# Layer 5's residual adds as accumulating DMAs in a deep-and-cross network, with later output transposes and x0 loads

## The chip, the core and the metric

The kernel runs on one core of a Trainium2 chip. The metric is the device time of one execution in microseconds (us). The core has TensorE (PE: matmuls; its weight loads are shown apart as PEld), VectorE (DVE), ScalarE (ACT), GpSimd (POOL) and SyncE (SP). In this kernel SP issues nearly all DMAs and POOL a few; 16 DMA engines carry them.

## The reference

```python
B, D, L = 16384, 1024, 6                       # bf16
x = x0
for l in range(L):
    proj = jnp.einsum('bd,de->be', x, ws[l]) + bs[l]
    x = x0 * proj + x
return x
```

Six layers. Each multiplies 16384 rows by a 1024 by 1024 matrix, adds a bias, multiplies by the untouched input x0 and adds x, the residual.

## The kernel before

**Tiles.** The 16384 rows go through in 16 pairs of 1024 rows (a pair is two blocks of 512, n = 0 and 1). A unit is one layer of one pair, 96 units in all, worked in the order pair 0 layers 0 to 5, pair 1 layers 0 to 5, and so on. x and x0 are held transposed in SBUF, features on the partitions: `x0Ts[pr % 2]` and `xsts[pr % 2]`, two buffers of each that the pairs use in turn. A quadrant (dh, n) of such a tile, `blk(t, dh, n)`, is 512 features of one block: 128 partitions by 2048 elements, 4 KB a partition, 512 KB.

**Fewer products.** A unit is a 2 by 2 block product done in Winograd's form with seven products. Differences of x are made by VectorE (T1 to T4), combinations of weight blocks ("5", "6", "7", "3", and inner ones "5i", "2i") too, but only in pair 0: POOL saves them to the DRAM tensor `Lc` (line 306) and later pairs load them from there. Pair 0 and the last unit use one level of this; all other units split two of the seven products again (`inner`, line 411).

**Evacuation.** TensorE sums into PSUM banks `pA[m]` and `pX[m]`. ScalarE moves them on: `F.m` copies pA[m] into pX[m], on which product 3 then builds (P3.m needs F.m); `E3.m` writes U, `E7.m` writes V, `E4.m` writes W, all with the bias (line 298); Q comes from E2 or from the inner products' copies (line 294). Q, U, V and W are tiles `ev2` to `ev5`, one buffer each, used again by every unit: the next unit's first E3 writes U's buffer again.

**Tail of a unit.** VectorE finishes each quadrant (line 202 is the helper `tt`): an add (Ua, Va), a product with x0 (Qm, Um, Vm, and Wma and Wmb in halves) and the residual add into xst (Qa, Ux, Vx, Wx; line 457). In the last unit of all, another branch finishes the quadrants in smaller pieces, with its own transposes and stores.

**Output and input of a pair.** After layer 5 SP transposes block n of xst into the same pair's x0T by DMA (`tro`, line 538), which needs both quadrants of block n (Q and W for n = 0, U and V for n = 1), and then stores x0T to `out` (`sto`, line 544). The next-but-one pair uses the same buffers. The x0 of the next pair is loaded into the other x0T by two transposing DMAs (`ld`, line 533).

**Order.** The program order of every engine is written by ranks. Each operation has a rank in us, its unit's base (23.4 us a unit, 24.2 in pair 0 and in the last) plus a number from a table (`EARLY` for the first units, `R2` for the rest). A heap takes the operation of lowest rank whose operands are already placed. Every engine runs its own list in that order, and waits by semaphores. Weights go through a ring of 16 tiles of 512 KB: after each placed operation, `pump` places as many loads on SP's list as the ring has free tiles, so an SP load waits for TensorE to finish with an old tile. A unit of pair 1 and later loads nine tiles.

Of the kernel before, what the change touches and what calls it, by code (L numbers as in the profile page):

```python
# [9 lines left out]
ADD = mybir.AluOpType.add  # L10
# [138 lines left out]
def kernel(  # L149
# [7 lines left out]
    nc = tc.nc  # L157
    P = nc.NUM_PARTITIONS
    B, D = x0.shape
    L = ws.shape[0]  # L160
# [3 lines left out]
    NB = 512  # L164
    PR = 2 * NB
    assert D == 1024 and B % PR == 0
    NPAIR = B // PR
# [15 lines left out]
    x0Ts = [work.tile([P, 2, KD, NB], BF16, name=f"x0T{i}") for i in range(2)]  # L183
# [5 lines left out]
    P1s, P5s, Q, U, V, W = (work.tile([P, KH, NB], BF16, name=f"ev{i}") for i in range(6))  # L189
# [8 lines left out]
    def blk(t, dh, n):  # L198
        return t[:, n, dh * KH:(dh + 1) * KH, :]

    def tt(o, a, b, op):
        nc.vector.tensor_tensor(out=o, in0=a, in1=b, op=op)  # L202
# [61 lines left out]
    def op(rank, fn, rd=(), wr=(), weights=()):  # L264
        for k in weights:
            uses_left[k] = uses_left.get(k, 0) + 1
        ops.append((rank, fn, tuple(rd), tuple(wr), tuple(weights)))

    base = 0.0
    QD = ((0, 0), (0, 1), (1, 0), (1, 1))  # L270
    for u, (pr, l) in enumerate(units):
        one, first, last = level1(u), u == 0, u == NU - 1
        rk = {**SAVES, **EARLY[u]} if u < len(EARLY) else (RLAST if last else R2)
        x0T, xst = x0Ts[pr % 2], xsts[pr % 2]
        xs = x0T if l == 0 else xst
        X0 = {q: f"x0.{pr % 2}.{q[0]}{q[1]}" for q in QD}
        XO = {q: f"xs.{pr % 2}.{q[0]}{q[1]}" for q in QD}
        XI = X0 if l == 0 else XO

        def add(name, fn, rd=(), wr=(), weights=(), rk=rk, base=base, u=u):  # L280
            op(base + rk[name], fn, rd, wr, [(u, w) for w in weights])

        def ttop(name, o, a, b, o_, rd, wr, **kw):
            add(name, lambda: tt(o, a, b, o_), rd, wr, **kw)
# [16 lines left out]
        if pr == 0:  # L301
# [32 lines left out]
            for X, s in (("2i", isum[2 * (l % 2)]), ("5i", isum[2 * (l % 2) + 1])):  # L334
                a = lambda r, c, X=X, u=u: wt[(u, X[0])][:, r * KQ:(r + 1) * KQ, c * HQ:(c + 1) * HQ]
# [37 lines left out]
        if not one:  # L373
            for X, Bm, src in (("5", T[1][:], "T1"), ("2", B21, XI[1, 0])):
                q = lambda dh, n, Bm=Bm: Bm[:, dh * KQ:(dh + 1) * KQ, n * NQ:(n + 1) * NQ]
# [15 lines left out]
        if not one:  # L391
            for X, Bm, src, a, b, C in (("5", T[1][:], "T1", 0, 1, P5s), ("2", B21, XI[1, 0], 2, 3, Q)):
                q = lambda dh, n, Bm=Bm: Bm[:, dh * KQ:(dh + 1) * KQ, n * NQ:(n + 1) * NQ]
# [50 lines left out]
        allm = lambda s: [f"{s}.{m}" for m in range(KH)]  # L444
        if not one:
            ttop("Q1", Q[:], Q[:], P1s[:], ADD, allm("Q") + allm("P1s"), allm("Q"))
        if not last:
            ttop("Ua", U[:], U[:], P5s[:], ADD, allm("U") + allm("5c"), allm("U"))
            ttop("Va", V[:], V[:], P5s[:], ADD, allm("V") + allm("5c"), allm("V"))
            for nm, C, q in (("Q", Q, (0, 0)), ("U", U, (0, 1)), ("V", V, (1, 1)), ("W", W, (1, 0))):  # L450
                if nm == "W":
                    for h, g in enumerate("ab"):
                        sl, ms = slice(h * KQ, (h + 1) * KQ), [f"W.{2 * h}", f"W.{2 * h + 1}"]
                        ttop("Wm" + g, C[:, sl], C[:, sl], blk(x0T, *q)[:, sl], MULT, ms + [X0[q]], ms)
                else:
                    ttop(nm + "m", C[:], C[:], blk(x0T, *q), MULT, allm(nm) + [X0[q]], allm(nm))
                ttop(nm + ("a" if nm == "Q" else "x"), blk(xst, *q), C[:], blk(xs, *q), ADD, allm(nm) + [XI[q]], [XO[q]])
        else:

# [24 lines left out]
            for m in range(KH - 1):  # L484
# [3 lines left out]
                out=W[:, KH - 1, :], in0=pA[KH - 1][:], scalar=b_all[:, c:c + 1], in1=blk(x0T, 1, 0)[:, KH - 1, :], op0=ADD, op1=MULT),  # L488
# [3 lines left out]
            for nm, src, dst, r, c0, c1 in outs:  # L492
                add("tr" + nm, lambda src=src, dst=dst: nc.sync.dma_start_transpose(
                    out=dst.rearrange("p j k r -> p (j k) r"), in_=src.rearrange("r j k p -> r (j k p)")),
# [30 lines left out]
        for f in late:  # L525
            f()
        nxt = pr + 1
        if l == (2 if pr == 0 else 0) and nxt < NPAIR:
            for n in range(2):
                XN = [f"x0.{nxt % 2}.{d}{n}" for d in range(2)]  # L530

                def ld(n=n, nxt=nxt):
                    nc.sync.dma_start_transpose(out=x0Ts[nxt % 2][:, n], in_=x0[nxt * PR + n * NB:nxt * PR + (n + 1) * NB, :])
                op(base + 23 + n, ld, [], XN)
        if l == L - 1 and not last:
            for n in range(2):
                def tro(n=n, x0T=x0T, xst=xst):
                    nc.sync.dma_start_transpose(out=x0T[:, n].rearrange("p k (j r) -> p (k j) r", r=P),
                                                in_=xst[:, n].rearrange("r k b -> r (k b)"))
                op(base + (28 if n == 0 else 31), tro, [XO[0, n], XO[1, n]], [X0[0, n], X0[1, n]])  # L540

                def sto(n=n, x0T=x0T, pr=pr):
                    with nc.allow_non_contiguous_dma(reason="256B runs"):
                        nc.sync.dma_start(out[pr * PR + n * NB:pr * PR + (n + 1) * NB, :].rearrange("(j p) (k r) -> p k j r", p=P, r=P),
                                          x0T[:, n].rearrange("p k (j r) -> p k j r", r=P))
                op(base + (42 if n == 0 else 45), sto, [X0[0, n], X0[1, n]], ["out"])
        base += SPAN0 if one else SPAN2


# [95 lines left out]
```

## Time and profile before

| | |
|---|---|
| median of 3 runs | 2271.25 us (2270.97 to 2272.67) |
| profiled execution: span from first to last instruction | 2269.4 us |
| TensorE busy | 2248.5 us, 99% of the span |
| VectorE busy | 2092.1 us, 92% |
| ScalarE busy | 1847.8 us, 81% |
| POOL busy | 24.5 us, 1% |
| mean granted TensorE clock | 1.000 |
| SP's DMA queue | 534.58 MB, 78.6% of 16 engines' span |
| POOL's DMA queue | 19.93 MB, 2.3% |
| weight load, issue to landing (median) | 4.7 us from Lc, 5.2 us from ws |
| Lc save by POOL, issue to landing (median) | 6.1 us and 6.8 us |
| output transpose, issue to landing (median) | 7.3 us |

The span leaves out what lies around the first and last instruction, 1.85 us against the median. In rows of the timeline the columns are the start in us, the length in us, the engine, the line, the operation, what is written and read, and the number of merged instructions; in brackets stands idle time before it and what ended it. A row of waits gives the total in us, the number and the longest. A window's row gives its length and the busy time of each engine, then the granted clock, the share of the DMA engines and their rate. Neighbouring instructions on an engine overlap a little, so from start to start a VectorE add takes 1.13 us where its own length is 1.22 us.

### The profile page before, as it was taken

The numbers are of one execution on the slowest core, as the hardware profiler recorded it, in microseconds if no ns is written. First come the engines' busy times: TensorE is split into PE (matmuls) and PEld (weight loads), VectorE is DVE, ScalarE is ACT, GpSimd is POOL, SyncE is SP. The second block draws the span as 40 slices with busy tenths as digits, with TensorE's granted clock in tenths as the row PEclk, the third lists the DMA queues.
The fourth block names the chain that finished last, engine by engine and source line by source line (L and its number), as shares of the span: only waits on it lengthen the run. The fifth ranks groups of instructions, "written<-read, shape, count | busy, mean of one in ns | idle before, by whom it ended". The sixth has DMA issues, their size and how long they took to land.

```text
span 2269.4 us, 34750 instructions
## 1 busy us (share of the span) xinstructions
PE 2248.5 (99%) x12754; PEld 1267.4 (56%) x12993; DVE 2092.1 (92%) x2331; ACT 1847.8 (81%) x3234; POOL 24.5 (1%) x46
## 2 busy tenths in 40 slices
PE   9999999999999999999999999999999999999998
PEld 4455555555555555555555555555555555555554
DVE  8999999999999999999999999999999999999997
ACT  6678888888888888888888888888888888888887
POOL 1110000000000000000000000000000000000000
PEclk9999999999999999999999999999999999999999
DMA  8779797796977969779697796977969689696872
GB/s 279 229 270 301 251 249 264 220 303 206 251 259 224 288 220 248 264 218 288 215 266 251 227 285 205 277 242 227 288 201 294 225 225 294 195 295 224 236 247 66
DMA packets 620492, 557.02 MB, mean 245 GB/s; under 512 B 391456, under 2 KB 546592, under 8 KB 620320
## 3 DMA queue, kind: packets, MB, share of 16 engines
q1 hardware_dynamic: 614240, 534.58, 78.6%
q0 software_dynamic: 5488, 19.93, 2.3%
q8 instruction: 102, 1.67, 0.3%
q14 instruction: 70, 0.57, 0.1%
q10 hardware_dynamic: 592, 0.27, 0.0%
HBM read 437.79 MB, written 52.43 MB: 216 GB/s over the span
## 4 chain that ended last, share of the span: by engine, by line
PE 99%; issue 1%; DMA 0%; ACT 0%; SPq 0%; DVE 0%; ACTq 0%
PE pA L289 58%; PE pX L411 24%; PE pX L289 17%; DMA ev<-in_x_dram 0%; ACT pX L294 0%; PE pA L505 0%; PE pX L359 0%; PE pX L505 0%; DVE x0T L516 0%; ACT ev L294 0%; ACT x0T L363 0%; ACT ip L294 0%; SPq L577 0%; SPq L574 0%; ACTq L294 0%
## 5 line engine op out<-in xcount | busy, mean ns | idle before, releaser
L289 PEld LDWEIGHTS <-wp 128*128 128x128 bf16 x7904 | 772.9, 98 | 838.1 <-issue 0.9
L289 PE MATMUL pA<-T,wp 128*128 128x512 bf16 x4468 | 1033.0, 379 | 7.3
L298 ACT ACTIVATE ev<-pA,b_all 128x512 bf16<-128x512 f32 x1123 | 717.5, 692 | 211.2 <-PE pA L289 164.0
L411 PEld LDWEIGHTS <-wp 128*128 128x128 bf16 x4984 | 487.7, 98 | 151.5 <-issue 0.2
L202 DVE TENSOR_TENSOR ev<-ev,x0T 128x2048 bf16<-128x2048 bf16 (+2 forms) x483 | 483.0, 1002 | 8.1 <-ACT ev L298 1.5
L202 DVE TENSOR_TENSOR ev<-ev,ev 128x2048 bf16<-128x2048 bf16 (+1 forms) x283 | 343.9, 1216 | 71.7 <-ACT ev L298 44.6
L202 DVE TENSOR_TENSOR xst<-ev,xst 128x2048 bf16<-128x2048 bf16 x319 | 389.1, 1220 | 19.1 <-PE pX L289 0.9
L411 PE MATMUL pX<-ti,wp 128*128 128x256 bf16 x2848 | 397.8, 273 | 0.0
L298 ACT ACTIVATE ev<-pX,b_all 128x512 bf16<-128x512 f32 x412 | 285.4, 697 | 63.8 <-PE pX L289 62.9
L289 PE MATMUL pX<-xst,wp 128*128 128x512 bf16 x1371 | 323.3, 379 | 0.3
L289 PE MATMUL pA<-xst,wp 128*128 128x512 bf16 x1205 | 302.4, 379 | 3.9
L294 ACT CAST ev<-pX 128x512 bf16<-128x512 f32 x384 | 232.1, 606 | 47.9 <-ACT ev L298 37.4
L294 ACT COPY pX<-pA 128x512 f32<-128x512 f32 x412 | 237.5, 602 | 21.7 <-PE pA L289 18.7
L294 ACT COPY pX<-pX 128x512 f32<-128x512 f32 x356 | 207.8, 584 | 8.6 <-ACT ip L294 0.2
L202 DVE TENSOR_TENSOR T<-xst 128x2048 bf16<-128x2048 bf16 x160 | 195.0, 1218 | 0.3
L202 DVE TENSOR_TENSOR T<-xst,T 128x2048 bf16<-128x2048 bf16 x160 | 195.0, 1219 | 0.2
L294 ACT CAST iu<-pX 128x512 bf16<-128x512 f32 x356 | 192.7, 601 | 0.0
L202 DVE TENSOR_TENSOR ev<-iu,ip 128x1024 bf16<-128x1024 bf16 x178 | 123.2, 692 | 60.7 <-ACT iu L294 60.7
L411 PE MATMUL pX<-T,wp 128*128 128x256 bf16 x1068 | 160.2, 273 | 0.0
L294 ACT CAST ip<-pX 128x512 bf16<-128x512 f32 x178 | 104.7, 589 | 54.0 <-PE pX L411 54.0
L411 PE MATMUL pX<-xst,wp 128*128 128x256 bf16 x888 | 133.2, 273 | 0.1
L202 DVE TENSOR_TENSOR xst<-ev,x0T 128x2048 bf16<-128x2048 bf16 x64 | 78.3, 1223 | 1.6
(50 smaller groups left out, 636.4 us busy)
## 6 DMA issues: line engine op xcount, KB each, us to landing
wp<-Lc SPq DMA_DIRECT2D x538, 512.0 KB, 4.7
wp<-in_ws_dram SPq DMA_DIRECT2D x287, 512.0 KB, 5.2
out_dram<-x0T SPq DMA_DIRECT2D x30, 1024.0 KB, 8.8
Lc<-wp POOLq DMA_DIRECT2D x24, 512.0 KB, 6.1
Lc<-isum POOLq DMA_DIRECT2D x12, 512.0 KB, 6.8
w<-in_ws_dram SPq DMA_DIRECT2D x5, 512.0 KB, 6.1
ev<-in_x_dram SPq DMA_DIRECT2D x3, 512.0 KB, 7.2
out_dram<-x0T SPq DMA_DIRECT2D x3, 256.0 KB, 4.2
```

Of the source, the lines that this page charges most:

```text
L202: nc.vector.tensor_tensor(out=o, in0=a, in1=b, op=op)
L289: nc.tensor.matmul(bank[:], lhsT=wt[(u, w)][:, k, m * P:(m + 1) * P], rhs=rhs[:, k, :], start=(start and k == 0), stop=(k == KH - 1), skip ...
L294: add(name, lambda: nc.scalar.copy(out=dst, in_=src), rd, wr)
L298: add(name, lambda: nc.scalar.activation(out=dst, in_=src, func=IDENT, bias=b_all[:, c:c + 1], scale=1.0), rd, wr)
L411: nc.tensor.matmul(pX[bank][:, m * NQ:(m + 1) * NQ], lhsT=wv[:, k, m * P:(m + 1) * P], rhs=rhs[:, k, :], start=(start and m == 0 and k == ...
```

## The change

In layer 5 of every pair but the last one, the residual add of each of the four quadrants is no VectorE instruction any more. POOL issues a DMA from the product tile (Q, U, V or W) onto the quadrant of xst, which adds as it writes (`accum_op=ADD`). It takes the rank of the add that it replaces. The two output transposes move from ranks 28 and 31 to 37 and 46, the two stores from 42 and 45 to 53 and 63. The two loads of the next pair's x0, which stood together in layer 2 (pair 0, ranks 23 and 24) or layer 0 (later pairs, ranks 23 and 24), are placed one in layer 2 and one in layer 3, at rank 23 of the layer in pair 0 and at rank 6 in later pairs.

```diff
@@ -454,6 +454,11 @@
                     ttop(nm + "m", C[:], C[:], blk(x0T, *q), MULT, allm(nm) + [X0[q]], allm(nm))
+                if l == L - 1:
+                    def accumulate(C=C, q=q, xst=xst):
+                        nc.gpsimd.dma_start(blk(xst, *q), C[:], accum_op=ADD)
+                    add(nm + ("a" if nm == "Q" else "x"), accumulate, allm(nm) + [XI[q]], [XO[q]])
+                    continue
                 ttop(nm + ("a" if nm == "Q" else "x"), blk(xst, *q), C[:], blk(xs, *q), ADD, allm(nm) + [XI[q]], [XO[q]])
@@ -525,25 +530,25 @@
-        if l == (2 if pr == 0 else 0) and nxt < NPAIR:
-            for n in range(2):
-                XN = [f"x0.{nxt % 2}.{d}{n}" for d in range(2)]
+        if l in (2, 3) and nxt < NPAIR:
+            n = l - 2
+            XN = [f"x0.{nxt % 2}.{d}{n}" for d in range(2)]
...
-                op(base + 23 + n, ld, [], XN)
+            op(base + (23 if pr == 0 else 6), ld, [], XN)
...
-                op(base + (28 if n == 0 else 31), tro, [XO[0, n], XO[1, n]], [X0[0, n], X0[1, n]])
+                op(base + (37 if n == 0 else 46), tro, [XO[0, n], XO[1, n]], [X0[0, n], X0[1, n]])
...
-                op(base + (42 if n == 0 else 45), sto, [X0[0, n], X0[1, n]], ["out"])
+                op(base + (53 if n == 0 else 63), sto, [X0[0, n], X0[1, n]], ["out"])
```

More of the change, by code (lines that the diff above doesn't have):

```diff
@@ L527, with ld @@
         nxt = pr + 1
-        if l == (2 if pr == 0 else 0) and nxt < NPAIR:
-            for n in range(2):
-                XN = [f"x0.{nxt % 2}.{d}{n}" for d in range(2)]
-                def ld(n=n, nxt=nxt):
-                    nc.sync.dma_start_transpose(out=x0Ts[nxt % 2][:, n], in_=x0[nxt * PR + n * NB:nxt * PR + (n + 1) * NB, :])
-                op(base + 23 + n, ld, [], XN)
+        if l in (2, 3) and nxt < NPAIR:
+            n = l - 2
+            XN = [f"x0.{nxt % 2}.{d}{n}" for d in range(2)]
+            def ld(n=n, nxt=nxt):
+                nc.sync.dma_start_transpose(out=x0Ts[nxt % 2][:, n], in_=x0[nxt * PR + n * NB:nxt * PR + (n + 1) * NB, :])
+            op(base + (23 if pr == 0 else 6), ld, [], XN)
         if l == L - 1 and not last:
```

## The prediction

> **What bounds the kernel now.** I read the chain that ended last first, because it says what sets the end, and then who made TensorE wait.
>
> ```profile
> PE 99%; issue 1%; DMA 0%; ACT 0%; SPq 0%; DVE 0%; ACTq 0%
> ```
>
> The chain is TensorE's own work nearly from end to end. The waits of the weight-load engine after the start-up are tiny:
>
> ```profile
> PEld L289 <- DVE T L202: 0.5, 1, 0.5
> ...
> PEld L289 <- DMA wp<-in_ws_dram: 0.4, 1, 0.4
> ```
>
> (Total us, times, longest.) TensorE hardly ever waits for VectorE or for a weight. In the timeline it runs one layer of 1024 rows in 23.38 us without a gap at a granted clock of 1.00. I found one late start outside start-up, at 1145.54 us, 0.19 us long, where a matmul follows VectorE's T2. So there is next to nothing to win, and whatever stops TensorE anywhere is added to the end, because no later slack repays it. The question is whether the change makes a new wait.
>
> **The change part by part.**
>
> *VectorE loses 60 adds* (15 pairs, 4 quadrants; pair 15 takes the other branch). One add takes 1.22 us, 73 us in all, but VectorE is off the path. The one stall of 0.19 us may go, since T2 comes about 2.3 us earlier: I take 0.2 us of gain.
>
> *POOL gains 60 DMAs of 512 KB, SBUF to SBUF, which add.* The trace has none. Its nearest row is the DMA queue of POOL: 5488 packets, 19.93 MB, 2.3% of 16 engines' span. That is 52 us for 38 transfers of 512 KB, 1.4 us each with the engines to itself. Below, an accumulate costs this much; reading the target as well as the source could double it to 2.7 us; 60 of them are 82 to 165 us of DMA time, beside a DMA share of 0.62 to 0.70 in the windows where they would run (1113.4 to 1136.8 and 1136.8 to 1145 us). That fits on average.
>
> The Trainium skill, "Collectives: The Full Stack", section on the bandwidth ceiling, speaks against the change here: a reducing DMA issues two reads per chunk and got half the rate of a copy. By it an accumulate is an estimated 2.7 us, the upper of my two; no run here shows it yet.
>
> *The new waits.* Before, Q, U, V and W (one buffer each) were free for the next unit when a 1.22 us add ended. Now they are free when the DMA has landed, and ScalarE's first write of each in the next unit waits for it. ScalarE works in order, so the copies behind that write wait too, and TensorE waits for those copies. For a pair boundary in the middle (around 1137 us) I set the end of each product against ScalarE's next write of its buffer: Q 1129.35 to 1144.95, U 1133.59 to 1150.12, W 1138.94 to 1159.13, V 1142.34 to 1155.68. The least margin is 13.3 us. POOL's transfers there would land as the page's 6.1 and 6.8 us, and 11.0 us at the slower end (below). **No wait at 14 boundaries.**
>
> **The first boundary (pair 0, layer 5) is different.** There VectorE still makes weight combinations and forms U last:
>
> ```profile
> 156.51 1.22 DVE L202 TENSOR_TENSOR ev<-ev,x0T 128x2048 bf16<-128x2048 bf16 x1
> ...
> 159.12 1.22 DVE L202 TENSOR_TENSOR xst<-ev,xst 128x2048 bf16<-128x2048 bf16 x1
> ...
> 162.66 1.82 DVE L202 TENSOR_TENSOR ev<-ev,x0T 128x1024 bf16<-128x1024 bf16 x2
> 164.40 2.35 DVE L202 TENSOR_TENSOR xst<-ev,xst 128x2048 bf16<-128x2048 bf16 x2
> ```
>
> (Start, length.) V's product, V's add, the second half of W's product with U's, the adds of W and U. U's product ends at 164.48. Without V's add (1.13 us from start to start) it ends at 163.35, and U's DMA is issued then. ScalarE's next use of U:
>
> ```profile
> 166.89 0.61 ACT L294 COPY pX<-pA 128x512 f32<-128x512 f32 x1
> 167.40 0.70 ACT L298 ACTIVATE ev<-pX,b_all 128x512 bf16<-128x512 f32 x1
> 167.98 0.61 ACT L294 COPY pX<-pA 128x512 f32<-128x512 f32 x1
> ```
>
> The row at 167.40 is E3.0, the first write of U in pair 1; the copy behind it is F.2. In the changed kernel's instruction order E3.0 waits for the semaphore of U's DMA and F.2 stands behind it. TensorE needs F.2 for the group that starts at 169.43:
>
> ```profile
> 168.56 1.03 PE L289 MATMUL pA<-T,wp 128*128 128x512 bf16 x4
> 169.43 0.81 PE L289 MATMUL pX<-x0T,wp 128*128 128x512 bf16 x3
> ```
>
> If U lands at T, F.2 ends 1.2 us later (0.58 us to F.2's start, 0.61 us of its own), so this group starts at T + 1.2: T - 168.2 late. F.3, two ScalarE rows further on, adds 0.2 us. The stall is T - 168.0.
>
> How long does U's DMA take? POOL's transfers in this stretch, from issue to landing, in two windows (161.8 to 162.5, and 144.5 to 148.2 us):
>
> ```profile
> Lc<-isum POOLq DMA_DIRECT2D x1, 512.0 KB, 7.3
> ```
>
> ```profile
> Lc<-wp POOLq DMA_DIRECT2D x4, 512.0 KB, 11.0
> ```
>
> The first had POOL's queue to itself, the others stood behind two more. The DMA share from 157 to 178 us is 1.10 at 390 GB/s: the engines are full, because SP is catching up with weight loads. U will stand behind V's DMA (157.7), a save of a weight combination (about 160.5) and W's DMA (162.2). So the nearest row is the one of 11.0 us: T = 163.35 + 11.0 = 174.3 and the stall is **6.3 us**. Ends: at the quietest landing in the trace (3.0 us) T = 166.4 and there is none; at 7.3 us it is 2.7; at the slowest landing of any DMA into x0T, 17.4 us, it is 12.8.
>
> Q's DMA takes a slot in the burst at 146.94, whose row landed in 11.6 us, at 158.5; ScalarE writes Q at 158.83. An accumulate at 2.7 us instead of 1.4 makes this about 1 us late. The wait for U, which counts from VectorE, swallows that.
>
> *The clock.* At the end of the trace the granted clock is still 1.00 from 2263.3 to 2268.5, after the last matmul, and 0.50 from 2268.6: a pause of some 5.2 us was followed by the half clock. At the start matmuls come 0.42 us apart from 1.2 us on for some 4 us, against 0.216 us later. A stall of 6.3 us may therefore cost up to 2 us more; nothing if the clock holds. I take 0.7.
>
> The Trainium skill, "TensorE: Matmul & The Clock Gate", section on what is actually happening, says one idle window of about 3.4 us, free-running, halves the clock. By it the loss would be likelier than I put it, an estimated 1.7 us.
>
> *SP's moved transfers.* Now SP spends 5.04 and 5.80 us on two output transposes at 1140.29 and 1146.04, waits before and behind two stores (8.27 and 5.12 us at 1157.40 and 1166.43) and needs 10.08 us for two x0 loads at 1171.65, in one run. Weight loads queue behind this, yet TensorE doesn't wait, because the ring of 16 holds some 30 us of work. The change puts weight loads between each, so less is late: no gain, no loss. The transposes now wait for DMAs: W issued at 1138.9 plus 11.0 is 1149.9, against rank 37, about 1150.7; were it 5 us late, SP's weight loads behind it would be 5 us late, inside the ring's cover. x0 arrives in layer 3 at the latest, about 60 us ahead of its pair. POOL's saves in pair 0 fall one or two slots back; their readers are a pair later.
>
> **Sum** on the profiled execution: span 2269.4, minus 0.2, plus 6.3, plus 0.7: 2276.2. The median of the runs is 1.85 us above the span (2271.25), so **2278.0**.
>
> **Rivals.**
> 1. *Hidden, not slower (0.28).* U lands before 172.7, that is within 9.3 us of its issue; the stall is at most 4.7 less the 0.2 gained, and the time lies between 2271.0 and 2275.8. For it: the 7.3 us row. Against it: V, W and a save ahead in the same queue.
> 2. *Slow accumulates, a wait at every boundary (0.10).* Four DMAs in a row, the first ready near 1133.4; V must land by 1155.7, so this begins at 5.5 us each, four times the copy price. At 7 us, V lands 5.7 us late, 15 times: about 2271 + 86 = 2357. Nothing in the trace excludes it; the doubled price is far from it.
> 3. *Faster (0.04).* If VectorE's port or lateness costs TensorE something that the profile hides: TensorE's idle is about 0.8 us in each window of 140.3 us, 12 us in 15; half of it would give 2265.
> 4. That the adds don't become DMAs is excluded: the changed order has 60 fewer on VectorE and 60 more on POOL.
>
> **Numbers.** Forecast (one stall of over 4.7 us at the first boundary): 0.58. No change means within 0.2%, 4.5 us, about what a measurement of this kernel can tell. Faster 0.04, same 0.28, slower 0.58 + 0.10 = 0.68. The range goes from 2271.0 (hidden) to 2290.0 (17.4 us landing, 2 us of clock, and some 4 us for a doubled price of the three accumulates ahead); outside lie rivals 2 and 3 and a little more. The forecast's own range is 2275.8 to 2290.0.
>
> **What will show it.** Right: a ScalarE wait for a DMA of xst near 167.4, U's landing near 174, one TensorE gap near 169 to 176, and all later layers at 23.38 us. Wrong: no gap there (rival 1), gaps at each boundary (rival 2), or SP late enough for weight waits.

## The result and the profile after

The changed kernel takes 2283.74 us, median of 4 runs (2283.06 to 2284.43), against 2271.11 us for the kernel before on the same chip (4 runs, 2270.54 to 2272.67). The ratio is 1.0056, with a 95% interval from 1.0042 to 1.007: slower by 12.6 us. The forecast was 2278.0 us (2271.0 to 2290.0), for the reason of one stall at the first pair boundary. The stall is there, alone and where it was expected, but it is larger than forecast.

The page of the kernel after (span 2282.2 us): busy time, POOL's DMA queue (packets, MB, share of 16 engines), the chain that ended last, by line, and the median landing of the new DMAs.

```profile
PE 2264.1 (99%) x12993; PEld 1267.7 (56%) x12993; DVE 2021.9 (89%) x2271; ACT 1848.0 (81%) x3234; POOL 76.0 (3%) x106
...
q0 software_dynamic: 14128, 51.39, 9.6%
...
PE pA L289 54%; PE pX L411 23%; PE pX L289 14%; DMA xst<-ev 1%; PE pA L510 0%; ACT pX L294 0%; PE pX L510 0%; DVE x0T L521 0%; ACT ev L294 0%; ACT ip L294 0%; ACT ev L298 0%; ACTq L298 0%
...
xst<-ev POOLq DMA_DIRECT2D x60, 512.0 KB, 7.9
```

VectorE has lost 70 us of work, as announced, and it bought nothing. New in the chain is a DMA onto xst with 1% of the span (0.7% with one more digit, 16 us): that is the size of one transfer of some 15 us, not of 60. Who waited for such a DMA, and for whom TensorE waited then, stands in the waits of the kernel after (us in total, times, longest):

```profile
ACT ev L298 <- DMA xst<-ev: 10.1, 1, 10.1
PE pX L289 <- ACT pX L294: 9.4, 2, 9.2
...
ACT ev L294 <- DMA xst<-ev: 2.0, 1, 2.0
PE pX L411 <- ACT pX L294: 1.1, 1, 1.1
```

60 DMAs, and exactly two waits for them by a compute engine. The second number of each row is what to read: a cost at every boundary would show 15 or 60 there. ScalarE's timeline of the kernel after shows the two places:

```profile
159.56 1.07 ACT L294 CAST ev<-pX 128x512 bf16<-128x512 f32 x2 [2.04 <-DMA xst<-ev]
...
167.48 0.61 ACT L294 COPY pX<-pA 128x512 f32<-128x512 f32 x1
178.16 0.69 ACT L298 ACTIVATE ev<-pX,b_all 128x512 bf16<-128x512 f32 x1 [10.07 <-DMA xst<-ev]
178.74 0.59 ACT L294 COPY pX<-pA 128x512 f32<-128x512 f32 x1
```

The first is Q's first write in pair 1, the second E3.0, the first write of U, and the row behind it is F.2. TensorE's timeline answers to it:

```profile
161.18 1.08 PE L411 MATMUL pX<-ti,wp 128*128 128x256 bf16 x8 [1.15 <-ACT pX L294]
...
169.16 1.03 PE L289 MATMUL pA<-T,wp 128*128 128x512 bf16 x4
179.38 3.57 PE L289 MATMUL pX<-x0T,wp 128*128 128x512 bf16 x8 [9.20 <-ACT pX L294]
182.75 8.20 PE L289 MATMUL pA<-T,wp 128*128 128x512 bf16 x32
```

So TensorE sits idle for 1.15 and 9.20 us, 10.3 us in all. POOL's timeline has the issues of the last saves, of V (157.49) and of W and U (the last row):

```profile
156.00 0.53 POOL L306 DMA_DIRECT2D Lc<-isum  x1 [5.65 <-DVE isum L202]
157.49 0.86 POOL L459 DMA_DIRECT2D xst<-ev  x1 [0.95 <-ACT pX L294]
159.88 0.55 POOL L306 DMA_DIRECT2D Lc<-isum  x1 [1.53 <-DVE isum L202]
161.87 1.75 POOL L459 DMA_DIRECT2D xst<-ev  x2 [1.44 <-ACT pX L294]
```

The last row ends at 163.62 and an issue of this kind takes 0.86 us, so U's DMA was issued at 162.76. Of POOL's DMAs, the issues of the kernel after in the window from 163.4 us on, which still holds the end of this one, have it alone:

```profile
xst<-ev POOLq DMA_DIRECT2D x1, 512.0 KB, 15.3
```

It landed at 162.76 + 15.3 = 178.06, and E3.0 started at 178.16. Windows of the kernel after (length, busy time of PE, PEld, DVE, ACT and POOL with instructions, granted clock, DMA share, GB/s) show what the clock did:

```profile
169.50:174.70 5.20, 0.68 (x4) 0.20 (x2) 3.05 (x4) 0.00 (x0) 0.00 (x0) 1.00 1.08 247
174.80:179.30 4.50, 0.00 (x0) 0.00 (x0) 0.00 (x0) 1.14 (x3) 0.00 (x0) 0.50 1.01 367
179.40:185.00 5.60, 5.60 (x14) 1.97 (x14) 1.25 (x2) 2.40 (x4) 0.00 (x0) 0.50 1.06 382
185.10:190.00 4.90, 4.90 (x24) 2.23 (x23) 4.06 (x4) 3.11 (x5) 0.00 (x0) 1.00 1.23 258
```

The clock is halved some 4.6 us after the end of the last matmul and is back about 5.6 us after the start of the next one. In these 5.6 us TensorE runs 14 matmuls where a full clock runs 26, so 12 matmuls of 0.216 us, 2.6 us, are late. Starts give the whole sum. The group behind the pause and the first matmuls of pair 1's layer 1, first in the kernel before and then in the kernel after (its group is the row of 179.38 above):

```profile
169.43 1.90 PE L289 MATMUL pX<-x0T,wp 128*128 128x512 bf16 x8
...
178.07 1.89 PE L289 MATMUL pA<-xst,wp 128*128 128x512 bf16 x8
```

```profile
190.78 1.89 PE L289 MATMUL pA<-xst,wp 128*128 128x512 bf16 x8
```

The start-up of the profiled execution after is 0.88 us shorter (TensorE's first L411 matmul on x0T of pair 1 starts at 154.66 against 155.54). The group behind the pause still starts 9.95 us later (179.38 against 169.43), so the two waits delay it by 10.8 us. From there to layer 1 it takes 11.40 instead of 8.64 us, 2.8 us more. Together, less the start-up, layer 1 begins 12.7 us later, and the span is 12.8 us longer. From pair 1's layer 1 to the last matmul the two need nearly the same time: 2085.1 to 2085.9 us in these two and in the first profile of each of the experiments 1 to 8.

### The profile page after: what moved, and what is told of

Read it like the earlier page. It is cut to its first block, busy times and chain, and to the rows that moved or that the text cites. A ratio compares the mean times of both kernels' runs of the same rounds, so it can differ in the third digit from the quotient of the medians.

```text
span 2282.2 us, 35141 instructions
## 1 busy us (share of the span) xinstructions
PE 2264.1 (99%) x12993; PEld 1267.7 (56%) x12993; DVE 2021.9 (89%) x2271; ACT 1848.0 (81%) x3234; POOL 76.0 (3%) x106
## 4 chain that ended last, share of the span: by engine, by line
PE 92%; DMA 1%; ACT 0%; issue 0%; DVE 0%; ACTq 0%
PE pA L289 54%; PE pX L411 23%; PE pX L289 14%; DMA xst<-ev 1%; PE pA L510 0%; ACT pX L294 0%; PE pX L510 0%; DVE x0T L521 0%; ACT ev L294 0%; ACT ip L294 0%; ACT ev L298 0%; ACTq L298 0%
## 5 line engine op out<-in xcount | busy, mean ns | idle before, releaser
L411 PEld LDWEIGHTS <-wp 128*128 128x128 bf16 x4984 | 487.6, 98 | 153.1 <-issue 1.9
L411 PE MATMUL pX<-ti,wp 128*128 128x256 bf16 x2848 | 397.9, 273 | 1.1 <-ACT pX L294 1.1
L202 DVE TENSOR_TENSOR xst<-ev,xst 128x2048 bf16<-128x2048 bf16 x259 | 315.8, 1219 | 15.4
L289 PE MATMUL pA<-xst,wp 128*128 128x512 bf16 x1280 | 313.5, 379 | 0.0
L411 PE MATMUL pX<-T,wp 128*128 128x256 bf16 x1068 | 160.2, 273 | 0.0
L411 PE MATMUL pX<-xst,wp 128*128 128x256 bf16 x888 | 133.2, 273 | 0.1
L459 POOL DMA_DIRECT2D xst<-ev x60 | 51.4, 857 | 1928.4 <-DVE ev L202 1601.2
```

The source lines that it names most:

```text
L289: nc.tensor.matmul(bank[:], lhsT=wt[(u, w)][:, k, m * P:(m + 1) * P], rhs=rhs[:, k, :], start=(start and k == 0), stop=(k == KH - 1), skip ...
L411: nc.tensor.matmul(pX[bank][:, m * NQ:(m + 1) * NQ], lhsT=wv[:, k, m * P:(m + 1) * P], rhs=rhs[:, k, :], start=(start and m == 0 and k == ...
L459: nc.gpsimd.dma_start(blk(xst, *q), C[:], accum_op=ADD)
```

## The experiments

Theory A: the whole loss is the stall at the first boundary, by U's buffer. Rivals: B, the moved transposes, stores and loads; C, a small cost at each of the 15 boundaries, by accumulates or by the DMA engines; D, the traffic at the first boundary, whoever waits for it. All diffs are against the changed kernel; "before" is the kernel before on the same chip. They are called run 1 to run 9 by their numbers here.

**1. Pair 0 keeps VectorE's adds.**

```diff
-                if l == L - 1:
+                if l == L - 1 and pr > 0:
```

> The changed kernel, but pair 0 keeps its four VectorE adds; pairs 1 to 14 add by DMA, and the transposes, stores and x0 loads stay where the change put them. Theory A (all of the 12.6 us comes from the first boundary: ScalarE waits there for the DMAs of Q and U, and the clock halves behind the pause): 2271, within 1 us of the kernel before. Theory B (the moved SP transfers cost the time): 2283.7, unchanged. Theory C (each of the 14 later boundaries pays a little for the DMA load): between, 2282 or so, 14/15 of the loss.

2270.42 us against 2270.64, ratio 0.9999 [0.999, 1.0009]. ScalarE has no wait for a DMA of xst left. 56 of the 60 accumulates with all moves cost nothing: C falls.

**2. The moves alone.**

```diff
-                if l == L - 1:
+                if False:
```

> The changed places of transposes, stores and x0 loads, and no accumulating DMA: all 60 adds are VectorE's again. A and C: 2271, as before. B: 2283.7.

2270.44 us, 0.9999 [0.999, 1.0009]. B falls; nor do the moves gain.

**3. Only U of pair 0 on VectorE.**

```diff
-                if l == L - 1:
+                if l == L - 1 and (pr > 0 or nm != "U"):
```

> The changed kernel, but in pair 0 the quadrant U alone is added by VectorE; Q, V and W of pair 0 stay DMAs. A: the wait of 9.2 us for U and the clock's loss go, the wait of 1.15 us of TensorE behind Q's DMA stays: 2272.3. A rival D, that the full DMA queue of that stretch delays something other than U's buffer (weights, the x0 of pair 1): 2280 or more, since three of four accumulates still run there. B: 2283.7.

2271.45 us, 1.0005 [0.9996, 1.0015]. One of 60 adds takes back 11.8 of the 12.6 us. In its waits one wait for a DMA of xst remains, that of Q, worth 1.1 us of TensorE:

```profile
ACT ev L294 <- DMA xst<-ev: 2.0, 1, 2.0
...
PE pX L411 <- ACT pX L294: 1.1, 1, 1.1
```

**4. All 60 accumulates, U of pair 0's layer 5 in a tile of its own.** This parts the buffer from the traffic (D): the DMA stays, and only nobody writes its source.

```diff
...
+        U = U_spare if u == L - 1 else U_main   # U_spare: a free tile of pair 0's weights
...
```

> The changed kernel with all 60 accumulating DMAs, but in pair 0, layer 5, U is written to a spare buffer (that of a weight tile which is free by then), so that the next unit's first write of U need not wait for the DMA. A: the DMA lands as late as before, near 178 us of the trace, and nobody waits for it but the output transpose: 2272.3, with Q's 1.15 us left. D, that the DMA traffic itself holds TensorE up: 2283.7. B: 2283.7.

2271.54 us, 1.0004 [0.9995, 1.0014]. U's DMA (here from the tile w) is as slow as ever, by the DMA issues around 163.5 us, and no compute engine waits for it (ScalarE's wait of 2.0 us for Q's stays):

```profile
xst<-w POOLq DMA_DIRECT2D x1, 512.0 KB, 15.3
```

This is the sharpest of the runs: same traffic, same landing, no loss. D falls; the price is the reuse of the buffer.

**5. A plain copy in place of the accumulate.** This leaves out the residual of layer 5.

```diff
-                        nc.gpsimd.dma_start(blk(xst, *q), C[:], accum_op=ADD)
+                        nc.gpsimd.dma_start(blk(xst, *q), C[:])
```

> The 60 DMAs copy instead of adding (the residual of layer 5 is left out): same bytes written, same waits, but the target isn't read. It tells how much of the late landing of U is the price of accumulating and how much the queue ahead. If an accumulate costs 2.8 us of the engines and a copy 1.4, U, behind Q, V and W, lands 4 to 6 us earlier, near 173 of the trace instead of 178; Q's wait goes, the pause is some 5 us and the time 2277 to 2278. If the queue of saves and weight loads is what makes it late: U lands as late as now, 2283 or so. If the price is all of it: no wait, 2271.

2280.66 us against 2270.6, 1.0042 [1.0027, 1.0056]. From its page, to be set against 9.6% and 7.9 us, and from its timeline:

```profile
q0 software_dynamic: 14128, 51.39, 5.9%
...
xst<-ev POOLq DMA_DIRECT2D x60, 512.0 KB, 5.5
```

```profile
174.88 3.57 PE L289 MATMUL pX<-x0T,wp 128*128 128x512 bf16 x8 [5.19 <-ACT pX L294]
```

The share of POOL's queue over that of before (2.3% of 2269.4 us), times the span, by 60: (9.6% x 2282.2 - 52) / 60 = 2.8 us of the 16 engines for an accumulate, (5.9% x 2279.1 - 52) / 60 = 1.4 us for a copy. The adding doubles the engine time. It makes U's landing 15.3 instead of 9.9 us and TensorE's pause 9.2 instead of 5.2. Landing and pause are as expected, but the time is 3 us above the 2277 to 2278 us. The half clock, 6.8 us long here, makes 2.9 us beside the pause: from the group behind it to layer 1 TensorE takes 11.55 us (174.88 to 186.43) against 8.64 in the kernel before. What else the expectation missed stays open.

**6. The pause filled with matmuls**, so that the clock stays up; run twice.

```diff
+        if u == L:
...
+            op(base + 13.25, busy, [], [Xn[2]])   # 35 matmuls of zeros into pX[2]
```

> The changed kernel with 35 extra matmuls of zeros (7.5 us) in pair 1, layer 0, into a PSUM bank that is free while TensorE waits for U's DMA, so that TensorE is busy in most of the pause. If the halved clock behind the pause costs about 3 us (the loss of 12.6 less the two waits of 10.4 and the start-up): 2280.6, and no half clock in the trace near 175 to 185. If the clock costs nothing there: 2283.7. If the extra matmuls get in the way: above 2284.

> The run with 35 extra matmuls in the pause again, with more runs, beside the changed kernel. The traces gave 1.6 to 2.5 us for the half clock (from start-up to the end of pair 1's first layer), the medians of few runs less than 1. If the traces are right: 2281. If the clock costs next to nothing on the whole: 2282.5 or more, within 0.7 of the changed kernel.

2282.57 us against 2270.6, 1.0052 [1.0037, 1.0067], and the second time 2282.64 against 2270.66, 1.0054 [1.0041, 1.0066]. The changed kernel beside the second:

> The changed kernel once more, on the same chip and beside the next run, as the measure for it: 2283.

2283.43 us, 1.0057 [1.0044, 1.0071]. In the first one's timeline the zeros fill most of the pause and the group behind them starts no earlier (179.49 against 179.38):

```profile
169.22 7.72 PE L437 MATMUL pX<-zeros 128*128 128x512 bf16 x35
...
179.49 2.12 PE L290 MATMUL pX<-x0T,wp 128*128 128x512 bf16 x8 [1.69 <-ACT pX L295]
```

The granted clock is 1.00 throughout. By the medians of one chip the half clock costs 2283.43 - 2282.64 = 0.8 us, where the expectations had 1.6 to 3; by the 12 late matmuls above, 2.6 us. The traces explain most of the difference. From the group behind the pause to the first matmul of layer 1, the filled executions take 8.86 and 8.87 us, the changed kernel 11.40 in its first profile and 10.07 (180.12 to 190.19) in its second, where the half clock lasted 6.8 instead of 10.2 us. So filling the pause saved 2.5 us against the one and 1.2 us against the other: part of the price is chance. But from the start of the last matmul to the end of the span both filled executions take 6.3 us, the two of the changed kernel 5.8 and 5.7, so half a microsecond of the saving is lost at the end. Why the end is longer there stays open.

**7. The accumulates alone, everything else at its old rank.**

```diff
-                op(base + (37 if n == 0 else 46), tro, ...)
+                op(base + (28 if n == 0 else 31), tro, ...)   # stores and x0 loads too
```

> The kernel before with the accumulating DMAs alone; transposes, stores and x0 loads stay at their old ranks. A: the moves pay for nothing and cost nothing, so 2283.7, within 2 us; SP waits some 7 us for W's DMA in front of the first transpose of each pair, inside the ring's cover of 14 us or more. Rival E, that the moves are needed because SP's wait holds up the weight loads: 2300 or more, with waits of TensorE for weights in layers 1 to 3 of the pairs.

2283.14 us, 1.0055 [1.004, 1.007], the same as with the moves. SP now waits for the accumulates, once in most boundaries, as the waits of SP in this run show:

```profile
SPq L543 <- DMA xst<-ev: 112.8, 14, 9.1
```

That is 8 us of SP each time, with weight loads queued behind it, and TensorE has no wait for a weight after the start-up in this run: the ring of weight tiles covers it. The moves avoid a wait that costs nothing.

**8. Accumulates in pair 0 only.**

```diff
-                if l == L - 1:
+                if l == L - 1 and pr == 0:
```

> The changed kernel, but only pair 0's four adds are DMAs; pairs 1 to 14 add on VectorE. A: 2283.7, the whole loss. C: 2272, one fifteenth of it. B: 2283.7, so B is told from A by the run of the moves alone.

2282.82 us, 1.0054 [1.0039, 1.0069]; U lands 15.25 us after its issue. Four of 60 accumulates make 12.2 of the 12.6 us: with run 1, the loss is told from both sides.

**9. Three saves of weight combinations put behind U's DMA**, to see how much of the landing is the queue.

```diff
+        if u == L - 2:
+            rk = {**rk, "s5i": 59.5}
+        if u == L - 1:
+            rk = {**rk, "s2i": 35.2, "s5i": 35.4}
```

> The changed kernel, but three saves of weight combinations in pair 0 (5i of layer 4, 2i and 5i of layer 5) are issued behind U's DMA instead of ahead of it; nothing else moves. In the changed kernel's trace these three take 1.7, 2.4 and 1.6 us of the landings between Q's and U's. If the queue ahead makes U late: U lands 5 to 6 us earlier, near 172, TensorE's pause is 3 to 4 us and the time 2276 to 2278. If the full engines (weight loads) or a fixed latency set it: U lands near 178 and the time stays at 2283.

2279.52 us (2278.37 to 2280.24) against 2270.66, 1.0038 [1.0024, 1.0052]. The DMA issues from 163.4 to 163.6 us hold U's alone, and TensorE's timeline has the shorter pause:

```profile
xst<-ev POOLq DMA_DIRECT2D x1, 512.0 KB, 10.7
```

```profile
175.13 3.37 PE L293 MATMUL pX<-x0T,wp 128*128 128x512 bf16 x8 [4.63 <-ACT pX L298]
```

Out of U's way, the three saves make its landing 4.6 us shorter (10.7 instead of 15.3): the queue ahead is worth about what its DMAs take, 1.7, 2.4 and 1.6 us for these three. The wait for Q stays (1.18 us). The time came down by about 4 us, not to the 2276 to 2278 us expected: U's landing was shortened by 4.6 us, not by 5 to 6, so the pause is 4.6 us and not 3 to 4, and the clock is halved after this pause as well, for 3.4 us.

No version beats the kernel before: runs 1 and 2 are equal to it within 0.1%.

## Why the prediction was right, and what it sized wrongly

**The mechanism was right.** It was read from two rows around 167.40 us: E3.0, and F.2 behind it in ScalarE's order. Both stand in the timeline after with the wait ahead of them, and runs 3 and 4 take the wait away and with it nearly all of the loss.

**The term that was mis-sized is U's landing**: 11.0 us taken, 15.3 us measured. The formula of the stall holds: with the landing of this execution, put into the time of the one before (its start-up is 0.88 us shorter), T is 178.9 and T - 168.0 gives 10.9, of which 0.2 are F.3's; the group behind the pause starts 179.38 + 0.88 - 169.43 = 10.8 us late. T came 4.6 us later than the forecast's 174.3. Of this 0.3 us is the issue: 163.35 was forecast, 162.76 + 0.88 = 163.64 came out, with the issue just behind that of W's DMA on POOL.

The rest is the queue. The prediction named V, a save and W ahead of U and took the row of saves that stood behind two others. It read 7.3 us as the landing of a transfer that had POOL's queue to itself. Both readings fall short. In the trace before, the save issued at 156.89 landed after 7.1 us, at 164.0, so the one of 161.91, which took the 7.3 us, still stood behind it. In the kernel after, V, the save at 159.88 and W took

```profile
xst<-ev POOLq DMA_DIRECT2D x1, 512.0 KB, 12.9
...
Lc<-isum POOLq DMA_DIRECT2D x1, 512.0 KB, 12.1
...
xst<-ev POOLq DMA_DIRECT2D x1, 512.0 KB, 13.1
```

and the saves issued at 147.16, 149.81 and 156.00 took 16.1, 15.2 and 11.4 us. Issue and landing added up, these six land at 163.3, 165.0, 167.4 (saves), 170.4 (V), 172.0 (save) and 175.0 (W), and U at 178.1. They land in the order of their issue, a save 1.6 to 2.4 us behind the transfer ahead of it and an accumulate some 3.0. So when U was issued, at 162.76, all six were still to land: the burst of saves that began at 144 had never drained. Run 5 measures the price of adding, 15.3 - 9.9 = 5.4 us of landing and 4.0 us of pause, about four times the 1.4 us by which an accumulate exceeds a copy (Q stands in the burst as well). Run 9 shows three of the saves ahead as another 4.6. The row of 11.0 us with 1.4 us more for each of V, W and U would come to 15.2, but that is partly luck, for this row had fewer transfers ahead of it. The price (1.4 to 2.7 us) was not carried into the landing of the forecast, only into the top of the range.

**The price of an accumulate** was put between 1.4 and 2.7 us; its top was right within 0.1. The Trainium skill, "Collectives: The Full Stack", section on the bandwidth ceiling, has a reducing DMA read twice and run at half the rate. The trace agrees: 2.8 us of engine time against 1.4 for the copy of run 5. Though the page speaks of a ring between cores, it was the better guide here than the copy's row; going by it, three doubled transfers would have made the forecast an estimated 4 us higher, near 2282.

**Q's wait** was said to be swallowed by U's. It was 2.0 us on ScalarE and 1.1 us of TensorE. In the changed kernel it does not add to U's stall, since U's lateness is counted from a DMA's landing; it appears by itself where U's is gone, 0.8 to 0.9 us above before in runs 3 and 4.

**The clock** was put at 0.7 us, "up to 2 more". Its sign is right. Against the 8.64 us of the kernel before, the stretch behind the pause is 1.4 to 2.8 us longer in the two traces of the changed kernel and those of runs 7 and 8: half of what is left of the half clock when the pause ends (2.9 to 5.6 us). The medians of run 6 give 0.8. The other page cited, "TensorE: Matmul & The Clock Gate" in the Trainium skill, section on what is actually happening, says that one idle window of about 3.4 us is enough. Here pauses of 4.6, 5.2 and 9.2 us halved it, and waits of up to 1.7 us (run 6) did not; no pause between these was tried.

**No wait at the 14 later boundaries**: right. There the accumulates landed 5.4 to 9.6 us after their issue, below the least margin of 13.3 us.

**SP's moves at zero**: right (run 2), and so was the cover by the ring (run 7).

**The gain of 0.2 us** from VectorE did not come. The stall of some 0.19 us at T2 comes and goes: four times in the profile after, at other layers, almost never in those of runs 1 and 2.

**Rival 2** has a slip in its sum. It starts its row of four DMAs at 1133.4, but by the prediction's own list Q's product is ready at 1129.35. So waits at every boundary would begin at 6.6 us a DMA, not 5.5, and at 7 us V would be 1.7 us late, not 5.7. Nothing else rests on it.

**Rival 3** rested on 0.8 us of TensorE idle in each window of 140.3 us. This idle time was never there. One window of 700 us of the kernel before, and the same stretch of the kernel after:

```profile
800.00:1500.00 700.00, 696.09 (x4000) 398.42 (x4072) 648.71 (x719) 579.21 (x1019) 0.00 (x0) 1.00 0.83 247
```

```profile
800.00:1500.00 700.00, 699.96 (x4073) 398.40 (x4072) 624.61 (x700) 579.09 (x1018) 17.13 (x20) 1.00 0.92 263
```

The weight loads agree (4072), the matmuls don't: in the trace before, 72 matmul records are missing, and 3.87 us of busy time with them. Over the whole run 12754 matmuls stand against 12993 weight loads there. The changed kernel's second profile (run 6) has 12754 too, and 2250.5 us of busy time where its first has 2264.1: it is the record that differs, not the kernel. So TensorE's busy time may not be compared between the pages before and after either (2248.5 and 2264.1), only its starts.

## What to carry to other kernels

An add that becomes a DMA holds its source until the landing, not until its issue: set each landing against the next write of that buffer, at the worst place (here the one boundary whose queue is full of saves), and follow what stands behind the writer in its engine's order. For that landing, add up what has not yet landed in the same queue, each at the price of its kind, twice for accumulates, rather than take a row of other transfers. Taking work off an engine that isn't the bound gives nothing, here some 70 us of it.

## What the runs showed of the hardware

- An accumulating transfer from SBUF to SBUF of 512 KB costs 2.8 us of the 16 engines against 1.4 us for a copy, lands after 7.9 against 5.5 us in the median, and POOL's issue of one takes 0.86 against 0.53 us.
- At the first boundary POOL's queue landed its DMAs in the order of their issue, and six transfers ahead made a landing of 15.3 us, against 5.4 to 9.6 us at the later boundaries.
- The half clock came in pieces of 3.4 us: three (10.2 us) after the pause of 9.2 us, in another execution of the changed kernel two (6.8 us) after the same pause, two after the one of 5.2 us and one after the one of 4.6 us. In the two executions of the changed kernel it cost 2.8 and 1.4 us, half of the 5.6 and 2.9 us of it that were left when matmuls started again. The same stall so costs a different time from one execution to the next.
- A trace can lose 2% of TensorE's matmul records evenly, and this looks like a steady small idle time; the count of weight loads beside it tells.
